# The first FFN product of chunks 16 to 19 as seven half products, in a kernel with its order written out by hand

## The chip, the cores and the metric

The kernel runs on one core of a Trainium2 chip. The time is in device microseconds (us) for one execution. Engines are named as the profile names them: PE (TensorE, matmuls), PEld (its weight loads), DVE (VectorE), ACT (ScalarE), POOL (GpSimd) and SP (SyncE, which here only issues DMAs).

## The reference

A linear attention with decay, then a feed-forward net with a squared ReLU:

```python
for t in range(S):                      # per batch and head, D = 64, S = 768
    state = gamma * state + outer(k[t], v[t])
    y[t] = scale * (q[t] @ state)
x = y, heads side by side               # 3072 tokens x 512
h = maximum(x @ w_in, 0)                # 512 x 2048
out = (h * h) @ w_out                   # 2048 x 512
```

There are 4 batches and 8 heads; inputs and output are float32, the matmuls take bf16.

## The kernel before

The 3072 tokens are 24 chunks of 128. Four chunks in a row form a group g (0 to 5), which shares an x tile `xt` (x transposed: 4 blocks of 128 rows x 512 tokens) and a tile of squares `h2` (16 blocks x 512 tokens).

Every step is given to a planner (`Plan.add`) with a name, and `TURNS` lists for each engine the order of all names. PE, DVE, ACT, POOL and SP each work through their list; a step waits on its engine until its inputs are there, and all behind it wait too. The planner gives the four PSUM banks `fps` in that order. The names:

- `ldk/ldq/ldv m` (SP, L701): loads of chunk m; `ck/cq m`: their casts to bf16 (L517 on ACT, L519 on DVE, L521 on POOL); `cv m` (DVE, L711): v with its decay; `X m` (SP, L743): DMA transpose of k and q.
- `V m.n` (PE, L767 to L805): a visit. It applies the state and scores for chunk m into the PSUM tile `yy`, and makes scores and state sums for chunk n in `sc`. Then `P n` (L846), `S n.0`, `S n.1` (L858, L856) and `Y m` (L866) on DVE make the masked scores, the new states and the x tile's columns.
- `F1.b.f` (PE, L979): eight 256-wide matmuls of the first FFN product for block b (two chunks), one bank; `R b.f` (ACT, L986) the ReLU to float32; `Q b.f` (L998 on ACT, L1000 on DVE) the square into `h2`. There are 16 of each for a group.
- `M1.c` to `M7.c` (PE, L1191): the second product for a unit of two chunks (c, c+1) as seven products of halves in the manner of Strassen and Winograd, eight matmuls each, in two banks (A, B). `H1, H2, H5, H6, H7` (DVE, L1166) are sums of squares for them, `e4, cc` (ACT, L1215, L1221), `t1, u1, w, c` (DVE, L1211) put the result together, and `st c.0`, `st c.1` (SP, L1245) store it. `w` frees bank A, `c` bank B.
- For the last group alone (chunks 20 to 23) the first product is done in that manner too (`ffn1_four`): `WI1` to `WI4` (L1032, two halves each) are sums of quarters of w_in, `TX0` to `TX3` (DVE, L1039) sums of x. For each tile t of four, `G1.t` to `G7.t` (PE, L1064) are four matmuls each; they go into two banks of `sc` or `yy` (U, W) and one of `fps` (V). `kc11, kc12, kc22` (ACT, L517) keep a product in float32, `c11, c22, c12` (DVE, L1079) add a second to it, `Qc..` squares the sum: one instruction on DVE (L1091), two on ACT (L1088 ReLU, L1089 square). `R.t` and `Q.t` (L1112, L1118) finish the fourth quarter. The w_in sums lie in the load buffers, the kept products in `yf`.

```python
            mult(2, "W", True)
            mult(1, "U", True)
            kept("c11", "U")
            both("c11", "W", bkeys["W"])
            squared("c11", 0, 0)
            mult(6, "U", False)      # adds to U after kc11 has read it
```

A half product that adds to a bank thus waits for the copy of what was there, and a first one for the bank to be freed.

Of the kernel before, what the change touches and what calls it, by code (L numbers as in the profile page):

```python
# [10 lines left out]
FP32 = mybir.dt.float32  # L11
BF16 = mybir.dt.bfloat16
# [6 lines left out]
class Plan:  # L19
# [47 lines left out]
    def schedule(self, nbanks, max_open, nslots):  # L67
# [176 lines left out]
BLOCKS = [2, 2, 1, 1, 2, 2, 2, 2, 2, 2, 2, 4]  # L244
# [27 lines left out]
FUSED = ()  # L272
# [80 lines left out]
def kernel(  # L353
# [9 lines left out]
    nc = tc.nc  # L363
# [22 lines left out]
    NLD, NBF, NQT, NXT, NH2, NWS, NOSB, NST = 4, 5, 5, 3, 3, 4, 3, 6  # L386
# [38 lines left out]
    osbs = [sb(f"osb{j}", [P, DM], FP32) for j in range(NOSB)]  # L425
    rts = [sb(f"r{j}", [P, 512], FP32) for j in range(NR)]
# [534 lines left out]
    def ffn1(blk):  # L961
# [4 lines left out]
        xt, h2, cols = xts[g % NXT], h2s[g % NH2], slice(u0 * C, u0 * C + n)  # L966
        for f0 in range(0, NFB, per):
# [22 lines left out]
            def relu_square(f0=f0, o1=o1):  # L990
                t = fps[o1["op"]["bank_index"]][:].rearrange("p (u n) -> p u n", u=per)
                nc.vector.scalar_tensor_tensor(out=h2[:, f0 : f0 + per, cols], in0=t, scalar=0.0, in1=t,
                                               op0=ALU.max, op1=ALU.mult)

            def square(on, f0=f0, o1=o1):
# [6 lines left out]
            hk = [f"h{g % NH2}.{u0 + w}.{f0 + u}" for u in range(per) for w in range(nb)]  # L1002
            i0 = pl.add(f"F1.{blk}.{f0}", "PE", per * NCB * (n * 0.4167 + (3 if n > C else 10)) / 1e3, reads, (f"g{grp}",), mm, lat=0.2, bank=("open", grp, False),
                        count=per * NCB, after=openers.get(g - NH2, ()))
            f1_of.setdefault(g, []).append(i0)
            o1["op"] = pl.ops[i0]
            if f"{blk}.{f0}" in FUSED:
                pl.add(f"RQ{blk}.{f0}", "DVE", 0.602, (f"g{grp}",), hk, relu_square,
                       bank=("close", grp), after=twin_users if g == NH2 - 1 else pt_users if g == 1 else ())
                continue  # L1010
# [3 lines left out]
                   after=twin_users if g == NH2 - 1 else pt_users if g == 1 else ())  # L1014

    def ffn1_four(blk):
        g = blk0[blk] // 4
        xt, h2 = xts[g % NXT], h2s[g % NH2]
        xk = [f"xt{g % NXT}.{u}" for u in range(4)]
        part = lambda k, t: xt[:, 2 * k : 2 * k + 2, 256 * t : 256 * t + 256]  # L1020
        ws = lambda h, k, j: w_in_bf[2 * h + j][:, 2 * k : 2 * k + 2, :]
        wkeys = lambda h, j: [f"win{2 * h + j}.{cb}.{e}" for cb in range(NCB) for e in range(2)]
        room = lambda x, slot: ld[x][:, slot, :].bitcast(BF16).rearrange("p (c n) -> p c n", c=2)
        places = {"1": ("k0", "k1"), "2": ("q0", "q1"), "3": ("v0", "v1"), "4": ("k2", "q2")}
        wt = {y + str(j): room(places[y][j][0], int(places[y][j][1])) for y in places for j in range(2)}
        for j in range(2):
            for y, a, b, op in (("1", (1, 0), (1, 1), ALU.add), ("2", "1", (0, 0), ALU.subtract),
                                ("3", (0, 0), (1, 0), ALU.subtract), ("4", (0, 1), "2", ALU.subtract)):
                ops_ = [wt[z + str(j)] if isinstance(z, str) else ws(*z, j) for z in (a, b)]
                reads = [x for z in (a, b) for x in ([f"WI{z}.{j}"] if isinstance(z, str) else wkeys(z[0], j))]  # L1030
                pl.add(f"WI{y}.{j}", WSUM2, 0, reads, (f"WI{y}.{j}", "ld" + places[y][j]),
                       lambda on, o=wt[y + str(j)], ops_=ops_, op=op: (nc.vector if on == "DVE" else nc.gpsimd).tensor_tensor(  # L1032
                           out=o, in0=ops_[0], in1=ops_[1], op=op), lock=BOTH)
        tx_ = xts[(g + 1) % NXT]
        tx = {y: tx_[:, 2 * (y // 2) : 2 * (y // 2) + 2, 256 * (y % 2) : 256 * (y % 2) + 256] for y in range(4)}
        for y, a, b, op in ((0, part(0, 1), part(0, 0), ALU.subtract), (1, part(1, 1), tx[0], ALU.subtract),
                            (2, part(1, 1), part(0, 1), ALU.subtract), (3, part(1, 0), tx[1], ALU.subtract)):
            pl.add(f"TX{y}", {"DVE": 0.341}, 0, xk + ([f"TX{y // 2}"] if y % 2 else []), [f"TX{y}"],
                   lambda on, y=y, a=a, b=b, op=op: (nc.vector if on == "DVE" else nc.gpsimd).tensor_tensor(  # L1039
                       out=tx[y], in0=a, in1=b, op=op), lock=BOTH, after=f1_of.get(g - 2, ()))  # L1040
        room32 = yf[:].rearrange("p a n -> p (a n)").rearrange("p (z y n) -> p z y n", z=2, y=3)
        left = {1: lambda f, k: ws(0, 0, f // 4)[:, k, C * (f % 4) : C * (f % 4) + C],
                2: lambda f, k: ws(0, 1, f // 4)[:, k, C * (f % 4) : C * (f % 4) + C],
                4: lambda f, k: ws(1, 1, f // 4)[:, k, C * (f % 4) : C * (f % 4) + C]}
        for i, y in ((3, "4"), (5, "1"), (6, "2"), (7, "3")):
            left[i] = lambda f, k, y=y: wt[y + str(f // 4)][:, k, C * (f % 4) : C * (f % 4) + C]
        right = {1: part(0, 0), 2: part(1, 0), 3: part(1, 1), 4: tx[3], 5: tx[0], 6: tx[1], 7: tx[2]}
        lkey = {1: lambda j: wkeys(0, j), 2: lambda j: wkeys(0, j), 4: lambda j: wkeys(1, j), 3: lambda j: [f"WI4.{j}"],
                5: lambda j: [f"WI1.{j}"], 6: lambda j: [f"WI2.{j}"], 7: lambda j: [f"WI3.{j}"]}
        rkey = {1: xk[:2], 2: xk[:2], 3: xk[2:], 4: ["TX3"], 5: ["TX0"], 6: ["TX1"], 7: ["TX2"]}  # L1050
        for t in range(4):
            z = t % 2
            both_ = held_by[z]
# [323 lines left out]
```

## Time and profile before

| what | value |
|---|---|
| time, median of three runs | 201.94 us (201.85 to 202.0) |
| the profiled execution | 202.31 us |
| its span, first to last instruction | 200.5 us |
| PE / PEld / DVE / ACT / POOL busy | 191.8 / 158.8 / 159.4 / 134.8 / 38.1 us |
| granted TensorE clock | 0.991 of full speed |
| bytes read and written | 27.26 and 6.29 MB |
| first product, chunks 0 to 19 (L979) | 704 matmuls |
| first product, chunks 20 to 23 (L1064) | 112 matmuls |

Busy times overlap, and a matmul's duration holds the depth of PE's pipeline, so durations of single matmuls must not be added up. The last product ends at about 197.1 us, and three DVE steps, a store and its landing follow.

### The profile page before, as it was taken

To read this page: it belongs to the slowest core of one execution; us is meant where nothing else is said; L and a number is where in the kernel's file an instruction comes from. 1 tells how busy PE (TensorE), PEld (TensorE's weight loads), DVE (VectorE), ACT (ScalarE), POOL (GpSimd) and SP (SyncE) were. 2 spreads that over 40 slices of the span, in tenths; PEclk is the share of its full clock that TensorE was granted. 3 is DMA by queue.
4 is the path that set the end of the run, shared out by engine and by line. 5 is a ranking of instruction groups with operands and counts; after the bars stand their busy time and mean duration, and the time that the engine had idled before them with its cause. 6 is when DMAs were issued, how large, how long until landed. Compare 5 with 4: busy or idle time off the path is not lost.

```text
span 200.5 us, 7020 instructions
## 1 busy us (share of the span) xinstructions
PE 191.8 (96%) x3011; PEld 158.8 (79%) x3016; DVE 159.4 (79%) x301; ACT 134.8 (67%) x239; POOL 38.1 (19%) x59
## 2 busy tenths in 40 slices
PE   8987999899999999999999999999999999999993
PEld 5654797674587888888888888888888888888882
DVE  3486449668849998969989888969899699999962
ACT  8564899778882784697885488386588418887601
POOL 6541352220102101201311012112010920000000
PEclk9996999999999999999999999999999999999999
DMA  5999999999999999999999999998992111100233
GB/s 158 290 312 320 345 345 336 352 264 215 245 162 241 207 248 204 256 170 250 128 146 243 205 246 214 210 225 191 157 194 54 56 56 56 52 0 28 83 105 105
DMA packets 97935, 38.46 MB, mean 192 GB/s; under 512 B 81008, under 2 KB 94320, under 8 KB 97904
## 3 DMA queue, kind: packets, MB, share of 16 engines
q1 hardware_dynamic: 97760, 37.89, 87.0%
q8 instruction: 23, 0.38, 0.8%
q10 hardware_dynamic: 144, 0.13, 0.2%
q14 instruction: 8, 0.07, 0.2%
HBM read 27.26 MB, written 6.29 MB: 167 GB/s over the span
## 4 chain that ended last, share of the span: by engine, by line
PE 65%; DMA 22%; SPq 6%; POOL 2%; issue 1%; ACT 1%; DVE 1%; DVEq 0%; POOLq 0%; ACTq 0%
PE fps L1191 27%; PE fps L979 21%; DMA kn<-in_k_dram 8%; DMA qkT<-kqs 7%; PE fps L1269 6%; DMA wst<-in_moe_w_in_dram 4%; DMA qn<-in_q_dram 4%; SPq L954 3%; PE yy L1064 2%; PE sc L1064 2%; SPq L536 2%; PE fps L1064 2%; PE yy L767 2%; PE sc L793 1%; PE yy L782 1%
## 5 line engine op out<-in xcount | busy, mean ns | idle before, releaser
L979 PE MATMUL fps<-xt,w_in 128*128 128x256 bf16 (+1 forms) x704 | 79.0, 266 | 0.9 <-ACT w_in L517 0.9
L979 PEld LDWEIGHTS <-w_in 128*128 128x128 bf16 x704 | 63.1, 99 | 9.4 <-ACT w_in L517 1.5
L986 ACT ACTIVATE r<-fps 128x512 f32<-128x512 f32 x80 | 47.1, 593 | 25.9 <-PE fps L979 19.8
L1191 PE MATMUL fps<-wst,h 128*128 128x256 bf16 x320 | 39.2, 273 | 0.0
L998 ACT ACTIVATE h<-r 128x512 bf16<-128x512 f32 x57 | 35.3, 628 | 1.1
L1191 PEld LDWEIGHTS <-h 128*128 128x128 bf16 x320 | 31.0, 98 | 3.9
L1191 PEld LDWEIGHTS <-wst 128*128 128x128 bf16 x240 | 23.3, 98 | 2.8
L711 DVE TENSOR_TENSOR vs<-vn,vf 128x512 bf16<-128x512 f32 x20 | 14.5, 724 | 7.4 <-DMA vn<-in_v_dram 7.4
L1166 DVE TENSOR_TENSOR wst<-h 128x1024 bf16<-128x1024 bf16 x30 | 19.4, 686 | 0.7 <-ACT h L998 0.4
L1191 PE MATMUL fps<-w_out,wst 128*128 128x256 bf16 x160 | 19.9, 273 | 0.0
L1000 DVE TENSOR_TENSOR h<-r 128x512 bf16<-128x512 f32 x23 | 16.2, 721 | 2.7 <-ACT r L986 2.7
L521 POOL CAST kqs<-kn 128x512 bf16<-128x512 f32 x12 | 8.4, 696 | 49.9 <-DMA kn<-in_k_dram 31.9
L521 POOL CAST kqs<-qn 128x512 bf16<-128x512 f32 x11 | 7.2, 653 | 43.6 <-DMA qn<-in_q_dram 30.9
L1269 PE MATMUL fps<-w_out,h 128*128 128x512 bf16 x59 | 14.4, 379 | 1.0 <-DVE w_out L519 0.6
L866 DVE TENSOR_TENSOR xt<-yy,yf 128x512 bf16<-128x512 f32 x19 | 13.1, 687 | 2.1 <-PE yy L782 1.9
L858 DVE TENSOR_TENSOR state<-sc,state 128x256 bf16<-128x256 f32 x33 | 13.8, 419 | 0.4
L1166 DVE TENSOR_TENSOR h<-h 128x1024 bf16<-128x1024 bf16 x20 | 13.7, 706 | 0.1
L846 DVE TENSOR_TENSOR pt<-sc,cmask 128x512 bf16<-128x512 f32 x20 | 13.6, 681 | 0.0
L1211 DVE TENSOR_TENSOR wu<-fps,wu 128x512 f32<-128x512 f32 (+1 forms) x16 | 9.1, 571 | 4.7 <-ACT osb L1221 2.5
L1221 ACT ACTIVATE osb<-fps 128x512 f32<-128x512 f32 x10 | 6.0, 596 | 8.6 <-PE fps L1191 8.6
L1269 PEld LDWEIGHTS <-h 128*128 128x128 bf16 x64 | 5.9, 98 | 6.8 <-issue 0.9
L1191 PE MATMUL fps<-wst,wst 128*128 128x256 bf16 x80 | 10.4, 273 | 0.0
(120 smaller groups left out, 245.3 us busy)
## 6 DMA issues: line engine op xcount, KB each, us to landing
qn<-in_q_dram SPq DMA_DIRECT2D x20, 256.0 KB, 5.0
kn<-in_k_dram SPq DMA_DIRECT2D x20, 256.0 KB, 5.6
vn<-in_v_dram SPq DMA_DIRECT2D x20, 256.0 KB, 5.5
out_dram<-osb SPq DMA_DIRECT2D x19, 256.0 KB, 3.8
wst<-in_moe_w_out_dram SPq DMA_DIRECT2D x4, 1024.0 KB, 10.2
wst<-in_moe_w_in_dram SPq DMA_DIRECT2D x4, 512.0 KB, 8.5
wst<-in_moe_w_in_dram SPq DMA_DIRECT2D x2, 1024.0 KB, 8.2
kn<-in_k_dram SPq DMA_DIRECT2D x2, 512.0 KB, 4.2
```

The lines of the kernel that those rows point to most:

```text
L521: nc.gpsimd.tensor_copy(o, t)
L711: lambda: nc.vector.tensor_tensor(out=o[:], in0=t.rearrange("s (h d) -> s h d", h=H), in1=vf[:, i, :, None].to_broadcast([P, H, D]), op=AL ...
L846: lambda: nc.vector.tensor_tensor(out=pt[:], in0=sc[:, :, 0:256].rearrange("s g (p t) -> s g p t", p=NJ), in1=cmask[:, None, None, :].to_b ...
L858: f = lambda cc=cc, j1=j1, j0=j0: nc.vector.tensor_tensor(out=sts[j1][:], in0=cc, in1=sts[j0][:], op=ALU.add)
L866: lambda: nc.vector.tensor_tensor(out=xt[:, :, u * C : u * C + C].rearrange("s p (g t) -> s g p t", g=2), in0=yy[:, :, 0:256].rearrange("s ...
L979: nc.tensor.matmul(ps[:, u * n : u * n + n], lhsT=w_in_bf[j][:, cb, c * P : (c + 1) * P], rhs=xt[:, cb, cols], start=(cb == 0), stop=(cb = ...
L986: nc.scalar.activation(o, t, AF.Relu)
L998: nc.scalar.activation(hv, rv, AF.Square)
L1000: (nc.vector if on == "DVE" else nc.gpsimd).tensor_tensor(out=hv, in0=rv, in1=rv, op=ALU.mult)
L1166: lambda on, o=a[name], x=a[x], y=a[y], op=op: (nc.vector if on == "DVE" else nc.gpsimd).tensor_tensor(out=o, in0=x, in1=y, op=op), lock=BOTH)
L1191: nc.tensor.matmul(ps[:, 256 * half : 256 * half + 256], lhsT=a[left][:, f], rhs=right(f), start=(first and f == 0), stop=True, skip_group ...
L1269: nc.tensor.matmul(ps[:, 0:w], lhsT=h2[:, fb, u * C : u * C + C], rhs=w_out_bf[j][:, c, ns], start=(fb == 0), stop=(fb == NFB - 1))
```

## The change

Chunks 16 to 19 are now one block of four too, so that `ffn1_four` runs for groups 4 and 5 (steps are named `G1.t.4`, `kc11.t.4` and so on, or `.5`). `F1`, `R` and `Q` of their two blocks of two go. In detail:

- For group 4, U and V are both banks of `fps`, and the second product goes to V rather than to a third bank W. The last group keeps U and W in `sc` and `yy`.
- The sums of w_in are made once and used for both groups. `WI1`, `WI2` and `WI4` lie in the tile of squares `h2[2]`, which held the squares of chunks 8 to 11; `WI3` overwrites its first operand in w_in. Group 4's kept products take the rest of that tile and one new tile, three places in turn. Group 5's squares go into `h2[0]` (`HOF`).
- There are two x tiles instead of three; three of the four sums of x have a new small tile, the fourth overwrites a quarter of x.
- From about the visit V15.16 on, the lists of all engines are written anew. All four chunks of group 4 must have been visited before most of its half products, and the visits stand earlier among the products. The casts of k and q of chunks 19 to 22 go to ACT, those of chunk 23 to POOL. Loads, transposes and stores on SP from ldk18 on have another order. The last two products of the kernel, M7.22 and M6.22, change places, and so do c1.22 and c2.22.

PE's list from V17.18 to V22.23, before and after:

```
V17.18 F1.8.10 M1.12 F1.8.12 F1.8.14 M4.12 F1.9.0 F1.9.8 M5.12 V18.19 F1.9.2 F1.9.4 M2.12 F1.9.6
F1.9.10 M6.12 M7.12 V19.20 F1.9.12 F1.9.14 M3.14 F1.10.0 F1.10.2 M4.14 F1.10.8 F1.10.6 V20.21 F1.10.10
F1.10.4 M1.14 M5.14 M2.14 F1.10.12 V21.22 F1.10.14 M6.14 M3.16 M7.14 V22.23

V17.18 M7.10 F1.8.0 F1.8.8 M4.12 F1.8.10 V18.19 F1.8.12 G1.0.4 M1.12 G2.0.4 M5.12 V19.20 M2.12 M6.12
G5.0.4 G6.0.4 M7.12 G3.0.4 G1.1.4 G7.0.4 M3.14 G2.1.4 G6.1.4 M4.14 G5.1.4 G4.0.4 G7.1.4 V20.21 G3.1.4
G4.1.4 M5.14 G1.2.4 G2.2.4 M2.14 M1.14 G5.2.4 G6.2.4 V21.22 G3.2.4 G1.3.4 G7.2.4 M6.14 G2.3.4 G6.3.4
M7.14 G5.3.4 G4.2.4 G7.3.4 V22.23
```

ACT's list after, from cc.12 to kc11.0.5, and SP's from ldk18 to ldk23:

```
cc.12 ck22 kc22.0.4 kc12.0.4 Qc11.0.4 kc11.1.4 Qc12.0.4 Qc22.0.4 kc12.1.4 e4.14 kc22.1.4 R.0.4 Qc11.1.4
Qc22.1.4 R.1.4 kc11.2.4 Qc12.1.4 Q.0.4 cc.14 kc22.2.4 kc12.2.4 Qc11.2.4 kc11.3.4 Qc12.2.4 Qc22.2.4
kc12.3.4 kc22.3.4 Qc11.3.4 Q.1.4 R.2.4 R.3.4 Q.2.4 Q.3.4 kc11.0.5

ldk18 ldq19 ldq18 X17 ldk19 ldk20 ldv18 ldq20 X18 ldv19 ldv20 X19 ldq21 st8.0 ldk21 X20 ldq22 ldk22
st10.0 ldv23 ldv21 ldv22 st10.1 X21 X22 ldq23 ldk23
```

The diff, cut to its core:

```diff
-BLOCKS = [2, 2, 1, 1, 2, 2, 2, 2, 2, 2, 2, 4]
+BLOCKS = [2, 2, 1, 1, 2, 2, 2, 2, 2, 4, 4]
+HOF = (0, 1, 2, 0, 1, 0)
...
-    NLD, NBF, NQT, NXT, NH2, NWS, NOSB, NST = 4, 5, 5, 3, 3, 4, 3, 6
+    NLD, NBF, NQT, NXT, NH2, NWS, NOSB, NST = 4, 5, 5, 2, 3, 4, 3, 6
...
+    txs = sb("tx", [P, 3, 2, 256], BF16)
+    spare = sb("spare", [P, 512], FP32)
...
-        xt, h2, cols = xts[g % NXT], h2s[g % NH2], slice(u0 * C, u0 * C + n)
+        xt, h2, cols = xts[g % NXT], h2s[HOF[g]], slice(u0 * C, u0 * C + n)
...
+    before = {g: max([x for x in range(g) if HOF[x] == HOF[g]], default=None) for g in range(NM // 4)}
+    fours = [x // 4 for x, n in zip(blk0, blocks) if n == 4]
+    ws = lambda h, k, j: w_in_bf[2 * h + j][:, 2 * k : 2 * k + 2, :]
+    wkeys = lambda h, k, j: [f"win{2 * h + j}.{2 * k + x}.{e}" for x in range(2) for e in range(2)]
+    room16 = h2s[2]
+    wt = {(y, j): room16[:, 4 * x + 2 * j : 4 * x + 2 * j + 2, :] for x, y in enumerate("124") for j in range(2)}
+    wt.update({("3", j): ws(1, 0, j) for j in range(2)})
+    wtkey = {(y, j): [f"WI{y}.{j}"] if y != "3" else wkeys(1, 0, j) for y in "1234" for j in range(2)}
+    room32 = [room16[:, 12 + 2 * x : 14 + 2 * x, :].rearrange("p a n -> p (a n)").bitcast(FP32) for x in range(2)] + [spare[:]]
+    room_last = yf[:].rearrange("p a n -> p (a n)").rearrange("p (x n) -> p x n", x=6)
+
+    def sums_of_w_in():
+        old = lambda *fs: [f"h2.{u}.{f}" for u in range(4) for f in fs] if HOF[2] == 2 else []
+        for j in range(2):
+            for x, y, a, b, op in ((0, "1", (1, 0), (1, 1), ALU.add), (1, "2", "1", (0, 0), ALU.subtract),
+                                   (2, "4", (0, 1), "2", ALU.subtract), (3, "3", (0, 0), (1, 0), ALU.subtract)):
+                ops_ = [wt[z, j] if isinstance(z, str) else ws(*z, j) for z in (a, b)]
+                reads = [k for z in (a, b) for k in (wtkey[z, j] if isinstance(z, str) else wkeys(*z, j))]
+                pl.add(f"WI{y}.{j}", WSUM2, 0, reads, wtkey[y, j] + (old(4 * x + 2 * j, 4 * x + 2 * j + 1) if y != "3" else []),
+                       lambda on, o=wt[y, j], ops_=ops_, op=op: (nc.vector if on == "DVE" else nc.gpsimd).tensor_tensor(
+                           out=o, in0=ops_[0], in1=ops_[1], op=op), lock=BOTH, after=twin_users if y != "3" else ())
+
+    turn32 = [0]
...
-        tx_ = xts[(g + 1) % NXT]
-        tx = {y: tx_[:, 2 * (y // 2) : 2 * (y // 2) + 2, 256 * (y % 2) : 256 * (y % 2) + 256] for y in range(4)}
+        tx = {0: txs[:, 0], 1: txs[:, 1], 2: part(0, 1), 3: txs[:, 2]}
...
-            pl.add(f"TX{y}", {"DVE": 0.341}, 0, xk + ([f"TX{y // 2}"] if y % 2 else []), [f"TX{y}"],
+            pl.add(f"TX{y}.{g}", {"DVE": 0.341}, 0, xk + {0: [], 1: ["TX0"], 2: ["TX0"], 3: ["TX1"]}[y], [f"TX{y}"],
...
-        room32 = yf[:].rearrange("p a n -> p (a n)").rearrange("p (z y n) -> p z y n", z=2, y=3)
...
+            if last:
+                z = t % 2
+                fixed = {"U": held_by[z][:, 0, :], "W": held_by[z][:, 1, :]}
+                bkeys = dict.fromkeys("UW", [("sc", "yy")[z] + x for x in "01"])
+            else:
+                fixed, bkeys = {}, {"U": [f"gU{g}.{t}"]}
+            bkeys["V"] = [f"gV{g}.{t}"]
...
+            c, ck, cold = {}, {}, {}
+            for x, name in enumerate(("c11", "c12", "c22")):
+                if last:
+                    c[name], ck[name], cold[name] = room_last[:, 3 * (t % 2) + x], f"last{3 * (t % 2) + x}", []
+                else:
+                    y = turn32[0] % 3
+                    turn32[0] += 1
+                    c[name], ck[name] = room32[y], f"room{y}"
+                    cold[name] = [f"h2.{u}.{12 + 2 * y + e}" for u in range(4) for e in range(2)] if y < 2 and HOF[2] == 2 else []
...
+            if last:
+                mult(2, "W", True)
+                mult(1, "U", True)
+                kept("c11", "U")
+                both("c11", "W")
+                squared("c11", 0, 0)
+                mult(6, "U", False)
+                kept("c12", "U")
+                mult(5, "V", True, True)
+                kept("c22", "V")
+            else:
+                mult(1, "U", True, True)
+                kept("c11", "U")
+                mult(2, "V", True, True)
+                both("c11", "V")
+                squared("c11", 0, 0)
+                mult(6, "U", False)
+                kept("c12", "U")
+                mult(5, "V", True)
+                kept("c22", "V")
...
+            while blocks[done] == 4 and before[m // 4] is not None and done2 < 4 * before[m // 4] + 4:
+                finish(done2)
+                done2 += 2
```

More of the change, by code (lines that the diff above doesn't have):

```diff
@@ L1000, in square @@
                     (nc.vector if on == "DVE" else nc.gpsimd).tensor_tensor(out=hv, in0=rv, in1=rv, op=ALU.mult)
-            hk = [f"h{g % NH2}.{u0 + w}.{f0 + u}" for u in range(per) for w in range(nb)]
+            hk = [f"h{HOF[g]}.{u0 + w}.{f0 + u}" for u in range(per) for w in range(nb)]
             i0 = pl.add(f"F1.{blk}.{f0}", "PE", per * NCB * (n * 0.4167 + (3 if n > C else 10)) / 1e3, reads, (f"g{grp}",), mm, lat=0.2, bank=("open", grp, False),
-                        count=per * NCB, after=openers.get(g - NH2, ()))
-            f1_of.setdefault(g, []).append(i0)
+                        count=per * NCB, after=openers.get(before.get(g), ()))
             o1["op"] = pl.ops[i0]
[L1007 to L1010, printed above, removed]
             i0 = pl.add(f"R{blk}.{f0}", RELU, 0, (f"g{grp}",), (f"r{grp}",), relu, bank=("close", grp), slot=("open", grp))
@@ L1016, in ffn1_four @@
+    turn32 = [0]
     def ffn1_four(blk):
         g = blk0[blk] // 4
[L1018 removed]
+        last = g == NM // 4 - 1
+        if g == fours[0]:
+            sums_of_w_in()
+        xt, h2 = xts[g % NXT], h2s[HOF[g]]
         xk = [f"xt{g % NXT}.{u}" for u in range(4)]
         part = lambda k, t: xt[:, 2 * k : 2 * k + 2, 256 * t : 256 * t + 256]
[L1021 to L1022 removed]
@@ L1023, in ffn1_four @@
[L1023 to L1033, printed above, removed]
@@ L1060, in mm, with at, mult @@
+            bkeys["V"] = [f"gV{g}.{t}"]
+            tag = f"{t}.{g}"
+            pool = lambda bank, end, tag=tag, fixed=fixed: None if bank in fixed else (end, (bank, tag), False) if end == "open" else (end, (bank, tag))
+            def at(bank, fixed=fixed, o1=o1):
+                return fixed[bank] if bank in fixed else fps[o1[bank]["bank_index"]][:]
+            def mult(i, bank, first, opens=False, t=t, at=at, bkeys=bkeys, o1=o1, tag=tag, pool=pool):
                 def mm():
-                    ps = banks[bank] if bank != "V" else fps[o1["op"]["bank_index"]][:]
+                    ps = at(bank)
@@ L1076, in both @@
-            def both(name, x, reads, t=t, c=c, banks=banks, o1=o1, **kw):
-                get = lambda: banks[x] if x != "V" else fps[o1["op"]["bank_index"]][:]
-                pl.add(f"{name}.{t}", "DVE", 0.602, reads, [f"{name}.{z}"],
-                       lambda: nc.vector.tensor_tensor(out=c[name], in0=get(), in1=c[name], op=ALU.add), **kw)
-            def squared(name, hh, tt, t=t, c=c):
+                i0 = pl.add(f"G{i}.{tag}", "PE", 0.437, lkey[i](t // 2) + rkey[i], bkeys[bank], mm, lat=0.2,
+                            count=4, bank=pool(bank, "open" if opens else "use"))
@@ new lines, in kept, with both @@
+            def kept(name, bank, c=c, ck=ck, cold=cold, at=at, bkeys=bkeys, tag=tag, pool=pool):
+                pl.add(f"k{name}.{tag}", KEPT, 0, bkeys[bank], [ck[name]] + cold[name],
+                       lambda on: copy_on(on, c[name], at(bank)), bank=pool(bank, "use"),
+                       after=y_made if last else twin_users)
+            def both(name, x, end="use", c=c, ck=ck, at=at, bkeys=bkeys, tag=tag, pool=pool):
+                pl.add(f"{name}.{tag}", "DVE", 0.602, bkeys[x], [ck[name]],
+                       lambda: nc.vector.tensor_tensor(out=c[name], in0=at(x), in1=c[name], op=ALU.add),
+                       bank=pool(x, end))
@@ L1120, in square @@
                     nc.vector.tensor_tensor(out=o, in0=rv, in1=rv, op=ALU.mult)
-            pl.add(f"Q.{t}", SQUARE, 0, (f"rw{t}",), [f"h{g % NH2}.{w}.{8 + 2 * t + u}" for u in range(2) for w in range(2)],
-                   square, slot=("close", ("f1w", t)), lock=BOTH)
+            pl.add(f"Q.{tag}", SQUARE, 0, (f"rw{tag}",), [f"h{HOF[g]}.{w}.{8 + 2 * t + u}" for u in range(2) for w in range(2)],
+                   square, slot=("close", ("f1w", tag)), lock=BOTH)
     def rows(m):
@@ L1262, in ffn2 @@
                 for j in range(4):
-                    reads = [f"h{g % NH2}.{u}.{4 * j + c}" for c in range(4)] + [f"wout{j}.{c}.{h}" for c in range(4) for h in range(2)]
+                    reads = [f"h{HOF[g]}.{u}.{4 * j + c}" for c in range(4)] + [f"wout{j}.{c}.{h}" for c in range(4) for h in range(2)]
                     def mm(j=j, o1=o1, h2=h2, u=u, ns=ns, w=w):
```

71 lines of the change are left out of this document (22 added, 49 removed), and 57 rows, old and new, of the table TURNS.

## The prediction

> **What bounds the kernel now.** I read the page first: its busy shares and its 40 slices.
>
> ```profile
> PE 191.8 (96%) x3011; PEld 158.8 (79%) x3016; DVE 159.4 (79%) x301; ACT 134.8 (67%) x239; POOL 38.1 (19%) x59
> PE   8987999899999999999999999999999999999993
> ```
>
> TensorE (PE) has no slice under 90% from the tenth on. A busy share can hide pipelining, so next comes the chain of waits in order of time (start, length, what), which gives the pace at which matmuls are really issued:
>
> ```profile
> 171.91 0.87 PE fps L1064 x8
> 172.78 0.44 PE yy L1064 x4
> 182.39 13.11 PE fps L1191 x120
> ```
>
> 13.11 / 120 = 109.3 ns for a matmul of 256 columns; eight take 0.874 us, four 0.437, whether they are the products of the second FFN (L1191) or of the half products (L1064). The mean durations in the page's groups (some 270 ns) hold the pipeline's depth and would make the saving 2.5 times too large. From 106 us to the last product PE's rows follow each other at this pace with no gap but the visits, 0.755 us each. So the end moves by what PE no longer does, unless PE begins to wait.
>
> The windows (PE, weight loads, DVE, ACT, POOL, clock, DMA) say who stands close behind it:
>
> ```profile
> 150.00:155.00 5.00, 5.00 (x80) 4.48 (x67) 4.96 (x11) 4.13 (x9) 0.08 (x1) 1.00 0.31 56
> 170.00:175.00 5.00, 5.00 (x48) 4.50 (x46) 4.58 (x8) 4.26 (x9) 0.00 (x0) 1.00 0.15 52
> ```
>
> VectorE (DVE) and ScalarE (ACT) are 85 to 99% busy where the half products of chunks 20 to 23 run. The clock is 1.00, so nothing is to be had there.
>
> **What the change removes.** The first product of chunks 16 to 19 is 16 groups of eight matmuls (128); seven half products for four tiles, four matmuls each, are 112. 16 x 109.3 ns = 1.75 us less on PE, all in the stretch without gaps. Early work is ordered as before up to about 108 us on every engine, so nothing moves there.
>
> [...]
>
> **What it adds.** For chunks 16 to 19, ACT and DVE had 16 ReLUs and 16 squares. Now they have 12 copies to keep a product, 12 additions, 12 squares of a sum, 4 ReLUs, 4 squares, and 4 sums of x. Prices, from ACT's timeline:
>
> ```profile
> 167.20 0.59 ACT L517 ACTIVATE yf<-yy 128x512 f32<-128x512 f32 x1
> 167.68 0.61 ACT L517 ACTIVATE yf<-sc 128x512 f32<-128x512 f32 x1
> 186.20 0.62 ACT L1088 ACTIVATE yf<-yf 128x512 f32<-128x512 f32 x1
> 186.86 0.63 ACT L1089 ACTIVATE h<-yf 128x512 bf16<-128x512 f32 x1
> 187.39 0.61 ACT L1088 ACTIVATE yf<-yf 128x512 f32<-128x512 f32 x1
> ```
>
> Start to start, a copy or ReLU from PSUM costs 0.485 us, a ReLU-and-square pair 1.19, a plain square 0.53; on DVE any 512-wide step starts 0.60 after the one before it. What ACT gains over the rest of the kernel is some 13.6 us, DVE 4 (it hands squares and a cast to ACT). None of this is on the path unless PE waits for it, so I laid PE's new order out without waits, from the visit V14.15 at 105.44 on, and asked at each place whether its inputs and its PSUM bank are there. A step of ACT starts 0.24 us after PE's last issue, one of DVE 0.15 (V17.18 ended at 127.87 by this count and its Y row began at 128.04).
>
> DVE: from V15.16 to V22.23 it has 38.9 us of steps in PE's 42.0 (before: 36.7 in 46.3). It waits for PE at several visits, so it holds.
>
> ACT is the tight one. From kc22.0.4 (it can start at 137.9, after G5.0.4) to Q.3.4 it has 16 copies and ReLUs (7.76), 10 pairs (11.90), 4 squares (2.12) and one 0.28: 22.06 us, to 159.96, its result about 160.1. M4.16, which reads that result, is due on PE at 160.35. ACT thus has no idle time for 22 us and arrives 0.2 us early. On the way kc12.3.4 is ready at 155.85, where G7.3.4 is due at 155.79: a wait of 0.1. G3.2.4 and G1.3.4 (the latter wants the bank that w.14 frees) have 0.1 to 0.2 to spare. I take 0.15 us of waits. The bounds: nothing, if copies overlap a little better; and 2 us, if each of the 21 copies and pairs in the run costs 0.1 us more than the dense rows (half a semaphore hop of PE to ACT).
>
> **The moved feed.** V18.19 is due on PE at 130.5 instead of 134.9, V19.20 at 134.7 instead of 141.7, because the half products need all four chunks. Each visit needs a transposed k and q by DMA:
>
> ```profile
> 121.26 2.13 SPq L743 DMA_TRANSPOSE qkT<-kqs  x1
> 127.75 1.91 SPq L743 DMA_TRANSPOSE qkT<-kqs  x1
> DMA to landing us min/median/max: 3.1/4.2/5.9
> ```
>
> These are X18 and X19, landing 4.3 and 4.2 later. SP is the issuer and runs into the DMA queue there: from ldk18 at 111.48 to X18 it passes nine issues, 1.09 us each, to X19 fourteen, 1.16 each. In the new order eight stand ahead of X18, eleven ahead of X19 and fifteen ahead of X20 (three stores and later loads go behind them). So X18 is issued at 120.2 to 120.8 and lands by 125.1, due 125.4; X19 lands by 128.5, due 130.5; X20 by 133.1, due 134.7. Cover shrinks from 1.6, 3.0 and 7 us to 0.3, 2.0 and 1.6. I take 0.1 us for X18; the slowest landing, 5.9, would make it 1.3. The casts of chunks 19 to 22 go from POOL to ACT; at those places ACT still has idle time (R8.0 would wait for PE anyway), and behind them stand ReLUs and copies of products that PE issues later. What waits for the delayed stores st8.0, st10.0 and st10.1 are the sums of units 12 and 14 into the same tiles, some 5 us later.
>
> **The weight sums** are eight as before, now needed from 137 on: five on DVE at 0.60 (in the DVE sum), three on POOL at 2.13, with the casts of chunk 23 behind them. POOL is done near 135 and those casts have until their loads come near 144; X23 then lands near 149, V22.23 is due 156.2. One DVE step (WI3.1) runs beside a POOL sum. The nearest rows:
>
> ```profile
> 148.84 0.67 POOL L521 CAST kqs<-kn 128x512 bf16<-128x512 f32 x1 [8.06 <-ACT h L998]
> 148.95 1.10 DVE L1032 TENSOR_TENSOR vn<-w_in,w_in 128x1024 bf16<-128x1024 bf16 x1
> 149.97 0.68 DVE L1032 TENSOR_TENSOR qn<-kn,w_in 128x1024 bf16<-128x1024 bf16 x1
> ```
>
> 0.42 us for the collision; TX0 behind it would be ready at 137.1, and G5.0.4 is due at 137.2: nothing, but without this cover it is 0.4. Two x tiles for three and the square tiles anew cost no wait: chunk 16's x overwrites what F1.6.14 read some 20 us earlier, and chunk 20's squares go where M7.14 reads last, before G2.0.5.
>
> **The tail.** The last two products change places, so the last store is issued by ACT, not SP. In the trace before, ACT's issue stood 0.23 us behind DVE's end, SP's 0.09: 0.15 more.
>
> **Sum.** -1.75 + 0.15 (ACT) + 0.10 (X18) + 0.15 (tail) = -1.35 us. The profiled execution took 202.31 (span 200.5 and 1.8 around it), 0.37 above the median; I carry the difference over: 201.94 - 1.35 = 200.6.
>
> **Rivals.** *ACT becomes the bound* (slower). Place: 138 to 160 us. ACT has 22.06 us for PE's 22.7, so every 0.03 us more on each of its 31 steps costs about 0.9 us, less the 0.2 to spare. At 0.1 on the copies and pairs PE waits 1.9 us more than forecast: 202.5. It is slower than before from 1.35 us of further waits on. For it: no stretch of the trace has ACT busy 22 us on end, and a late copy holds PE at once, since the next half product adds into the same bank. Against it: its dense runs keep their 0.485 and 1.19.
>
> *The feed is late.* If X18 to X20 land no earlier than before (125.6, 131.9, 134.6), V18.19 waits 1.4 us, and what follows has that as slack: 200.6 + 1.3 = 201.9, no change. A landing of 5.9 at X19 on top gives 203.
>
> *PE is not the bound.* If PE could issue faster than it does and something beside it set the pace, the 16 matmuls would be worth nothing and the added 0.4 us would stay: 202.3. The even 109.3 ns through products of both kinds speaks against it. [...]
>
> **How the numbers follow.** Forecast 0.74; ACT bound 0.14; late feed 0.08; PE not the bound 0.04. This kernel's runs lie within 0.15 us, so about 0.2% (0.4 us) is what can be told from no change: faster is under 201.54, slower over 202.34. Faster is the forecast alone, 0.74. The late feed gives 0.05 to no change and 0.03 to slower, PE not the bound 0.03 and 0.01, and the ACT bound is slower: same 0.08, slower 0.18. The forecast's own range is 200.1 (no waits, no tail cost) to 201.4; the range that leaves out no more than 2 in 10 reaches into the ACT case, to 202.6.
>
> **What would show it.** In the profile after: 112 matmuls in place of 128 for these chunks, PE's issue pace still 109.3 ns; the last product's end near 195.6 instead of 197.1; V19.20 near 135; ACT without idle time from 138 to 160. Gaps of PE released by ACT between 143 and 160 would show the ACT rival, gaps at visits released by the transposes near 125 to 135 the feed. Wrong would be any PE wait over half a us, or a pace that changes.

## The result and the profile after

The changed kernel takes 200.66 us (median of 22 runs, 199.92 to 204.75) beside 201.94 (22 runs, 201.48 to 203.78) of the kernel before on the same chip: a ratio of 0.9937 with a 95% interval of 0.9917 to 0.9958, 1.28 us less. Now and then an execution takes well over a per cent longer than the others of its kernel, as the 204.75 did; the ratios leave out such executions, the medians do not. The profiled execution took 200.48 us (span 198.7), 1.83 less than the one of before.

The page of the changed kernel, its busy line and PE's, DVE's and ACT's slices:

```profile
PE 189.6 (95%) x2995; PEld 157.0 (79%) x3000; DVE 160.9 (81%) x309; ACT 145.4 (73%) x262; POOL 34.1 (17%) x54
PE   8886999999999999999999999999999999999993
DVE  3486439777849898978999479989999998999962
ACT  8564789968882684687887868498999999798101
```

PE has 16 instructions fewer and is still full from the fifth slice to the last but one. ACT's busy time grew by 10.6 us, and its slices read 9 where group 4's half products run.

The chain of waits (start, length, what) answers to the pace shown before, and it holds the only wait of PE between 125 us and the last product that the kernel before has not:

```profile
153.95 0.87 PE fps L1226 x8
154.82 0.45 PE fps L1080 x4
155.28 0.03 ACTq L524
155.30 0.44 ACT h L524
155.75 0.04 issue
155.79 0.60 PE fps L1080 x4
180.60 13.12 PE fps L1226 x120
```

The pace has not changed: 13.12 / 120 = 109.3 ns. L1080 are the half products, L1226 the second product. At 155.79 begins G7.3.4. Four matmuls at that pace from about 155.10 would have let it begin at 155.54, so PE stood for 0.25 us behind a copy of ACT (L524, kc12.3.4). On ACT's timeline that copy (155.16) stands behind the pair Qc22.2.4; the two rows above it are the square of Qc11.2.4 and the copy kc11.3.4, which the account of ACT further down needs:

```profile
151.63 0.63 ACT L1114 ACTIVATE h<-h 128x512 bf16<-128x512 f32 x1
152.29 0.60 ACT L524 ACTIVATE h<-fps 128x512 f32<-128x512 f32 x1
...
153.98 0.61 ACT L1113 ACTIVATE spare<-spare 128x512 f32<-128x512 f32 x1
154.62 0.63 ACT L1114 ACTIVATE h<-spare 128x512 bf16<-128x512 f32 x1
155.16 0.58 ACT L524 ACTIVATE h<-fps 128x512 f32<-128x512 f32 x1
```

The windows (PE, weight loads, DVE, ACT, POOL, clock, DMA share, GB/s), first of the kernel before:

```profile
138.00:149.00 11.00, 11.00 (x160) 9.72 (x159) 10.11 (x18) 7.71 (x16) 1.39 (x3) 1.00 0.96 180
149.00:160.00 11.00, 11.00 (x230) 9.39 (x232) 9.26 (x19) 7.75 (x14) 5.58 (x4) 1.00 0.32 70
```

and of the kernel after:

```profile
138.00:149.00 11.00, 11.00 (x160) 9.71 (x159) 10.88 (x21) 10.78 (x21) 1.74 (x2) 1.00 0.90 167
149.00:160.00 11.00, 10.91 (x227) 9.15 (x224) 10.85 (x21) 10.84 (x22) 0.00 (x0) 1.00 0.35 93
```

ACT went from 15.46 to 21.62 us of 22, as forecast. DVE went from 19.37 to 21.73: it is as full as ACT.

**One stretch for every comparison.** Executions differ ahead of the change as well: V14.15's scores began at 105.93 us in the profile of before, at 105.61 in that of after, at 105.05 to 108.07 in the experiments. I therefore measure from there to the start of the last of the 256-wide matmuls. That stretch took 91.03 us before (196.96 - 105.93, with 768 such matmuls) and 89.56 after (195.17 - 105.61, with 752). The 1.47 us are 16 x 109.3 ns = 1.75, less 0.25 for G7.3.4, less 0.03 that lies at the visits, whose lengths differ by some hundredths. The other 0.36 of the 1.83 lie ahead of V14.15 (0.32) and behind the last matmul (0.04).

### The profile page after: what moved, and what is told of

Same layout as the page of the kernel before. It is cut to its first block, busy times and chain, and to the rows that moved or that the text cites. A ratio compares the mean times of both kernels' runs of the same rounds, so it can differ in the third digit from the quotient of the medians.

```text
span 198.7 us, 7019 instructions
## 1 busy us (share of the span) xinstructions
PE 189.6 (95%) x2995; PEld 157.0 (79%) x3000; DVE 160.9 (81%) x309; ACT 145.4 (73%) x262; POOL 34.1 (17%) x54
## 4 chain that ended last, share of the span: by engine, by line
PE 74%; DMA 16%; SPq 5%; POOL 1%; DVE 1%; issue 1%; ACT 1%; DVEq 0%; ACTq 0%
PE fps L1226 30%; PE fps L986 20%; DMA kn<-in_k_dram 8%; PE fps L1080 8%; PE fps L1304 6%; DMA wst<-in_moe_w_in_dram 4%; DMA qkT<-kqs 4%; SPq L961 3%; PE yy L1080 2%; PE sc L1080 2%; PE yy L774 2%; SPq L543 2%; PE yy L789 1%; PE sc L800 1%; PE sc L812 1%; POOL w_in L528 1%
## 5 line engine op out<-in xcount | busy, mean ns | idle before, releaser
L986 PE MATMUL fps<-xt,w_in 128*128 128x256 bf16 (+1 forms) x576 | 62.9, 263 | 1.3 <-ACT w_in L524 1.1
L993 ACT ACTIVATE r<-fps 128x512 f32<-128x512 f32 x64 | 37.3, 591 | 16.0 <-PE fps L986 15.4
L1226 PE MATMUL fps<-wst,h 128*128 128x256 bf16 x320 | 40.1, 273 | 0.0
L1226 PEld LDWEIGHTS <-h 128*128 128x128 bf16 x320 | 30.9, 98 | 3.9
L1000 ACT ACTIVATE h<-r 128x512 bf16<-128x512 f32 x48 | 29.6, 626 | 0.9
L1226 PEld LDWEIGHTS <-wst 128*128 128x128 bf16 x240 | 23.3, 98 | 2.8
L1226 PE MATMUL fps<-w_out,wst 128*128 128x256 bf16 x160 | 20.3, 273 | 0.0
L718 DVE TENSOR_TENSOR vs<-vn,vf 128x512 bf16<-128x512 f32 x20 | 13.9, 699 | 5.8 <-DMA vn<-in_v_dram 5.7
L1002 DVE TENSOR_TENSOR h<-r 128x512 bf16<-128x512 f32 x16 | 11.2, 709 | 3.7 <-ACT r L993 3.7
L528 POOL CAST kqs<-kn 128x512 bf16<-128x512 f32 x10 | 6.9, 691 | 41.9 <-DMA kn<-in_k_dram 36.1
L1080 PEld LDWEIGHTS <-w_in 128*128 128x128 bf16 x128 | 12.5, 98 | 1.7 <-issue 0.3
L1201 DVE TENSOR_TENSOR h<-h 128x1024 bf16<-128x1024 bf16 x20 | 13.6, 702 | 0.0
L853 DVE TENSOR_TENSOR pt<-sc,cmask 128x512 bf16<-128x512 f32 x20 | 13.6, 680 | 0.0
L528 POOL CAST kqs<-qn 128x512 bf16<-128x512 f32 x8 | 4.9, 613 | 36.6 <-DMA qn<-in_q_dram 36.6
```

The source lines that it names most:

```text
L528: nc.gpsimd.tensor_copy(o, t)
L718: lambda: nc.vector.tensor_tensor(out=o[:], in0=t.rearrange("s (h d) -> s h d", h=H), in1=vf[:, i, :, None].to_broadcast([P, H, D]), op=AL ...
L853: lambda: nc.vector.tensor_tensor(out=pt[:], in0=sc[:, :, 0:256].rearrange("s g (p t) -> s g p t", p=NJ), in1=cmask[:, None, None, :].to_b ...
L986: nc.tensor.matmul(ps[:, u * n : u * n + n], lhsT=w_in_bf[j][:, cb, c * P : (c + 1) * P], rhs=xt[:, cb, cols], start=(cb == 0), stop=(cb = ...
L993: nc.scalar.activation(o, t, AF.Relu)
L1000: nc.scalar.activation(hv, rv, AF.Square)
```

## Experiments

Theory: PE issues without a gap, so its 16 matmuls are the gain; one place behind ACT gives 0.25 of it back. Rivals: ACT or DVE sets the time between 138 and 160 us; the feed of X18 to X20 does; PE's matmuls are worth less than their pace; the tail costs something. All times are medians; ratios are against the kernel before on the same chip.

**The changed kernel again.**

> The changed kernel once more, as the measure for the others of this set on the same chip. Both theories: 1.3 us under the kernel before (ratio 0.9937), one wait of PE at G7.3.4 of about 0.25 us, released by ACT.

200.78 us (8 runs), ratio 0.9923 (0.9896 to 0.9949). The result stands. The profile is of an execution of 203.90 us: it has the wait at G7.3.4 (0.25), but also two that the first profile has not, of 0.2 us at V17.18 (X18 landed at 127.99) and 0.76 at V19.20 (X20 at 138.12), in a stretch of 90.50. Most of what it took longer came ahead: its V14.15 began at 108.07.

**The matmuls back, and nothing else.** In each first half product that opens a bank, the opening matmul is issued twice: 16 more matmuls with their weight loads, no more work for the other engines.

```diff
-    nc.tensor.matmul(...)
+    for _ in range(2 if first and u == 0 and k == 0 and (not last or i == 2) else 1):
+        nc.tensor.matmul(...)
```

> 16 matmuls more: the first matmul of each opening half product of group 4 (12) and of G2 of group 5 (4) is issued twice, so that PE has as many 256-wide matmuls as before the change. Theory (PE's pace is the bound): 16 x 109.3 ns = 1.75 us slower than the changed kernel, less the 0.25 us of the wait at G7.3.4 that the later PE no longer meets: 1.5 to 1.75, so 0.1 to 0.5 us slower than the kernel before. Rival (PE is not the bound, something beside it sets the pace): under 0.5 us slower than the changed kernel.

202.06 us (12 runs), ratio 0.9989 (0.9970 to 1.0008): the gain is gone, with 1.28 us more than the control in the medians. The stretch is 91.05 us, 1.49 more than after: 1.75 less the 0.25 at G7.3.4, which no longer occurs because ACT has time to come. Its chain ends on PE at the same pace:

```profile
181.72 13.12 PE fps L1227 x120
```

So a matmul costs its pace here, and PE is the bound. Weight loads are busy for 9.71 of 11 us (88%) in the first window of after above, and still the run shows no headroom on PE.

**The copy first.** On ACT, kc12.3.4 goes ahead of the ReLU and square Qc22.2.4.

```diff
-Qc12.2.4 Qc22.2.4 kc12.3.4 kc22.3.4
+Qc12.2.4 kc12.3.4 Qc22.2.4 kc22.3.4
```

> ACT's list: kc12.3.4 goes ahead of the pair Qc22.2.4, all else as in the changed kernel. Theory (PE's pace sets the time, and ACT, which has no idle time from 138 to 160 us, costs one wait): kc12.3.4 is ready 1.2 us earlier, the wait of 0.25 us at G7.3.4 goes, nothing new is late (kc22.3.4 then ends where it did), 0.2 to 0.25 us faster than the changed kernel, last product at 195.0 instead of 195.3. Rival (ACT bounds the whole stretch): the work of ACT is the same, so the wait comes back later in the stretch, at M4.16 at the latest, and the time stays within 0.05 us.

200.40 us (6 runs), ratio 0.9913 (0.9885 to 0.9941), 0.4 under the changed kernel on the same chip, with intervals that overlap. The expected 0.20 to 0.25 is only in part there: on PE's timeline G7.3.4 begins without a wait, and a smaller one of 0.11 stands behind the visit V22.23 (four matmuls at 157.41, the next at 157.97 instead of 157.86):

```profile
155.80 0.60 PE L1080 MATMUL fps<-tx,w_in 128*128 128x256 bf16 x4
156.23 0.60 PE L1080 MATMUL fps<-xt,w_in 128*128 128x256 bf16 x4
...
157.41 0.61 PE L1080 MATMUL fps<-xt,h 128*128 128x256 bf16 x4
157.97 0.60 PE L1080 MATMUL fps<-tx,w_in 128*128 128x256 bf16 x4
```

So the move gains 0.14 at these two places. This execution's stretch is longer all the same, 90.61, by two waits for the feed: 0.27 at V17.18, whose scores want X18 (issued 120.28, landed 125.13), and 0.92 at V19.20, whose scores (L800) want X20 (the row counts the idle time alone, 0.76):

```profile
135.46 0.32 PE L800 MATMUL sc<-qkT 64*64 64x64 bf16 x16 [0.76 <-DMA qkT<-kqs]
```

**More work for ACT.** One square of group 4 (Q.0.4) is done twice on ACT.

```diff
-    nc.scalar.activation(o, rv, AF.Square)
+    for _ in range(2 if tag == "0.4" else 1):
+        nc.scalar.activation(o, rv, AF.Square)
```

> ACT squares Q.0.4 twice: one step of 0.53 us more in the stretch where ACT has no idle time. Theory (ACT is full there, arriving 0.1 to 0.2 us ahead of PE at most places): PE waits 0.4 us at G3.2.4 and the wait at G7.3.4 grows with it, 0.5 us slower than the changed kernel in all. Rival (ACT has slack there and the wait at G7.3.4 has another cause): no change, within 0.1 us.

201.36 us (12 runs), ratio 0.9963 (0.9942 to 0.9984), 0.6 more than the control beside it. The two squares took ACT 1.18 us to the next step's start, where the one took 0.52: 0.66 more, and not the 0.53 of the expectation.

```profile
149.38 1.27 ACT L1154 ACTIVATE h<-r 128x512 bf16<-128x512 f32 x2
150.56 0.58 ACT L1257 ACTIVATE osb<-fps 128x512 f32<-128x512 f32 x1
```

PE's timeline has it at two places, after the visit V21.22 and at G7.3.4:

```profile
151.67 0.60 PE L1080 MATMUL fps<-xt,h 128*128 128x256 bf16 x4 [0.55 <-ACT spare L524]
...
156.81 0.60 PE L1080 MATMUL fps<-xt,w_in 128*128 128x256 bf16 x4 [0.18 <-ACT h L524]
```

Counted from start to start, the first holds PE 0.61 longer than a visit otherwise does, and the second is 0.34 instead of 0.25. Its stretch is 91.15 us: 89.56 + 0.61 + 0.09 + 0.90 (to 0.01), the last a wait for X20 at V19.20 as in the run before. So ACT has nothing to spare: 0.66 us more of work costs 0.70.

**More work for DVE.** One of the 1024-wide additions for unit 14, H5.14, is done twice, which takes DVE 0.72 us more from start to start.

```diff
-    nc.vector.tensor_tensor(out=o, in0=x, in1=y, op=op)
+    for _ in range(2 if name == "H5" and c0 == 14 else 1):
+        nc.vector.tensor_tensor(out=o, in0=x, in1=y, op=op)
```

> DVE makes H5.14 twice: one step of 0.60 us more near 143 us. The prediction's reading (DVE's sum to V22.23 is 38.9 us of PE's 42, it holds): at most 0.3 us slower than the changed kernel, by c22.1.4 ahead of G4.1.4, which has 0.35 us to spare, and nothing later. Rival (DVE is busy 21.8 of 22 us from 138 to 160 and is a second full engine there): 0.5 to 0.6 us slower.

200.61 us (12 runs), ratio 0.9953 (0.9925 to 0.9980): no measurable difference to the changed kernel. In the trace DVE's addition c22.1.4 begins 0.61 us later than in the changed kernel, both counted from V14.15, and G4.1.4 waits for it:

```profile
145.32 0.60 PE L1080 MATMUL fps<-tx,w_in 128*128 128x256 bf16 x4 [0.25 <-DVE spare L1103]
```

PE loses 0.41 there by its starts, the wait at G7.3.4 is gone since ACT gains that time, and the stretch is 89.74, 0.18 more. DVE is as busy as ACT but is late less: at this place it had some 0.2 (0.61 - 0.41) to give, where ACT has none.

**A late feed.** SP issues X19 after the loads that stood behind it.

```diff
-ldv20 X19 ldq21 st8.0 ldk21 X20
+ldv20 ldq21 st8.0 ldk21 X19 X20
```

> SP's list: ldq21, st8.0 and ldk21 go ahead of X19 instead of behind it. Theory (the loads and transposes pass the DMA queue at about 1.1 us each and have little cover left): X19 lands 3.3 us later, near 132.2, V18.19 is due at 130.3, so PE waits about 1.9 us there; X20 follows at once and lands near 133.3 to 134, so V19.20 does not wait more; 1.7 to 2.0 us slower than the changed kernel, slower than the kernel before. Rival (the feed still has the cover of before, 3 us and more): no change.

202.28 us (12 runs), ratio 1.0027 (0.9991 to 1.0063). The profiled execution is the fastest of them (201.0). Counted from V14.15, X19 was issued 2.3 us later than in the changed kernel (124.84 - 105.05 against 123.07 - 105.61), and V18.19 waited 1.10 us from start to start:

```profile
131.04 0.32 PE L800 MATMUL sc<-qkT 64*64 64x64 bf16 x16 [0.92 <-DMA qkT<-kqs]
```

Its stretch is 90.65, which is 89.56 + 1.10 to 0.01. A transpose 2.3 us later thus takes 1.1 us in the trace and 1.5 in the medians (202.28 against the control's 200.78), all of the gain; the expected 1.7 to 2.0 was more. The rival of the late feed is a real one: the changed kernel's own cover is enough in some executions and not in others.

**The tail as before.** M7.22 and M6.22, and c1.22 and c2.22, back in their old order.

```diff
-... w.22 c2.22 c1.22          # DVE
-M6.22 M7.22                   # PE
+... w.22 c1.22 c2.22
+M7.22 M6.22
```

> The last two products and the two DVE steps behind them in the order of before (M7.22, M6.22; c1.22, c2.22), all else as in the changed kernel. The prediction's term for the tail: 0.15 us faster than the changed kernel, since SP issues the last store 0.09 us behind DVE, ACT 0.23. Rival (the trace after shows 0.67 us from the last product to the last store, 0.66 before): no change, within 0.05 us.

200.84 us (12 runs), ratio 0.9951 (0.9925 to 0.9978), no difference. The timelines' last two store issues, of before, of after and of this run, one fence for each:

```profile
197.41 0.37 ACTq L1238 DMA_DIRECT2D out_dram<-wu  x1
197.74 0.34 SPq L1238 DMA_DIRECT2D out_dram<-wu  x1
```

```profile
195.61 0.34 SPq L1273 DMA_DIRECT2D out_dram<-wu  x1
195.95 0.37 ACTq L1273 DMA_DIRECT2D out_dram<-wu  x1
```

```profile
195.49 0.37 ACTq L1273 DMA_DIRECT2D out_dram<-wu  x1
195.82 0.34 SPq L1273 DMA_DIRECT2D out_dram<-wu  x1
```

The second issue begins 0.33 or 0.34 after the first, whichever queue comes first: each follows 0.02 to 0.04 us behind the end of its DVE step (197.38 and 197.71 before, 195.59 and 195.91 after), and those two steps are that far apart. The last issue stands 0.78 us behind the start of the last matmul in all three (197.74 - 196.96, 195.95 - 195.17, 195.82 - 195.04).

**An earlier feed.** X20 was late in three profiles (the control's, the copy's and that of more work for ACT), so SP issues it ahead of a store.

```diff
-X19 ldq21 st8.0 ldk21 X20
+X19 ldq21 X20 ldk21 st8.0
```

> The changed kernel with one move on the queue of SP: the transpose X20 and the load of chunk 21's k go ahead of a store (st8.0, 1.92 us of issue), so X20 is issued at about 125.7 instead of 128.2 and the k load at its old time. Theory (the shorter feed cover costs part of the executions: V19.20's scores wait 0.8 to 0.9 us for X20 in some, nothing in others): that wait is gone in every profile, executions without it keep their time, and the median comes down by 0.1 to 0.5 us, to 200.2 to 200.6. Rival (the spread between executions is of the chip, and X20 only shows it): the median stays at 200.7 to 200.8, and another wait stands in the place of V19.20's. Against the move: the store is issued 2.5 us later; where the sum of unit 12 into its tile waits for it, ACT or DVE stops near 134 and PE loses up to 1 us.

200.82 us (6 runs), ratio 0.9934 (0.9908 to 0.9959): no gain. X20 was issued at 125.6 and landed at 130.7, due 134.8; the stretch is 89.55. The store pays for it: st8.0, issued at 129.07, landed at 132.87, and t1.12, which overwrites the tile that it reads, began at 132.97, 0.88 us after e4.12 instead of the 0.41 in the changed kernel. PE lost no more than 0.04 behind that.

**The earlier feed and the copy first.** Both moves together.

> The same move on SP's queue, and on ACT the copy kc12.3.4 one place earlier, ahead of the ReLU and square Qc22.2.4. If both waits that the trace of the changed kernel shows (0.25 us at G7.3.4, 0.8 to 0.9 at V19.20 in part of the executions) are of these two places, the median is 0.3 to 0.6 us below the changed kernel's, 200.1 to 200.5, with no wait over 0.15 us on PE between 125 us and the last product. Rival (the work of ACT and DVE is the limit between 138 and 160 us, so that what one place gains the next loses): no more than 0.1 us below the feed alone.

201.71 us (12 runs), ratio 0.9965 (0.9938 to 0.9993), a miss. Its profile is of an execution of 204.88 us, and it shows what the move can do. On DVE's timeline t1.12 waits for the store:

```profile
131.49 0.68 DVE L853 TENSOR_TENSOR pt<-sc,cmask 128x512 bf16<-128x512 f32 x1
135.98 0.42 DVE L1246 TENSOR_TENSOR osb<-fps,e 128x256 f32<-128x256 f32 x1 [3.81 <-DMA out_dram<-osb]
```

st8.0 was issued at 130.27 there. PE's next second product wants the bank that t1.12 and the step after it free, so PE stood too, and then something else followed. The row of PE, and its windows (busy, clock, DMA share, GB/s):

```profile
136.46 1.03 PE L1226 MATMUL fps<-w_out,wst 128*128 128x256 bf16 x8 [2.60 <-DVE osb L1246]
```

```profile
134.00:136.40 2.40, 0.00 (x0) 1.00 1.00 210
136.40:138.00 1.60, 1.54 (x71) 0.95 1.00 244
138.00:141.20 3.20, 3.20 (x35) 0.50 1.14 254
141.20:144.00 2.80, 2.80 (x27) 0.99 0.88 120
```

After 2.60 us without a matmul, and 1.4 us after the matmuls had come back, the granted clock fell to 0.50 for 3.41 us (137.83 to 141.24; the windows above cut it at both ends), and matmuls came each 213 ns. The stretch of 94.05 is 4.6 us over that of the best run below: 2.76 for the wait, 1.58 for the clock and 0.27 for X18 at V17.18, all from start to start. Whether this is why the median is higher is not shown, since the other executions have no trace; the move was not used again.

**The changed kernel a third time.**

> The changed kernel itself, on the same chip as the two kernels with the earlier feed: 200.5 to 200.8 us if its earlier medians (200.66, 200.78) hold here. By the theory of the feed some of its executions show a wait of 0.8 to 0.9 us at V19.20; a profile of one execution shows it or not.

200.74 us (11 runs), ratio 0.9934 (0.9914 to 0.9954). The profiled execution took 201.56, yet its stretch is 89.56 with no wait but the one at G7.3.4: all of the 1.1 us that it is slower than the first profile came ahead of V14.15.

**The feed ordered anew, with the store early.** The store goes ahead of X20, chunk 21's loads behind, and their casts on ACT later.

```diff
-X19 ldq21 st8.0 ldk21 X20                      # SP
+X19 st8.0 X20 ldq21 ldk21
-Q8.8 cq21 e4.12 R8.12 kc11.0.4 Q8.10 ck21 Q8.12 cq22   # ACT
+Q8.8 e4.12 R8.12 kc11.0.4 Q8.10 Q8.12 cq21 ck21 cq22
```

> The changed kernel with chunk 20's feed ahead of chunk 21's, and the store before both: SP's order is X19, st8.0, X20, ldq21, ldk21; on ACT the casts cq21 and ck21 stand after Q8.12, where their loads will have come. X20 is issued near 127 instead of 128.2, and st8.0, whose landing releases the tile that t1.12 writes near 132.4, at 125 to 126 in place of 125.7 to 128. Theory (part of the executions lose time at these two covers, 0.55 to 2.1 us for X20 and 0.55 to 0.8 for st8.0): no wait at V19.20, t1.12 never held by the store, and the median 0.1 to 0.4 us under the changed kernel's 200.66 to 200.78. Rival (the executions' spread comes from elsewhere, much of it already from before 60 us): the median stays within 0.1 of 200.7. Against it: ldq21 lands near 134, and if the casts hold ACT past 137.4 the first copy of the half products is late, and ACT carries that for 20 us: 201 to 201.5.

200.91 us (12 runs), ratio 0.9949 (0.9923 to 0.9975). X20 landed at 132.3, due 136.0, so its cover is 3.7 us, and there is no wait at V19.20 or for the store. The stretch is 89.66, and the execution (201.87) lost 1.1 us at V14.15, whose X15 came late; that place is as before the change. The rival is right: what the executions differ by is not made at X20 alone, and the median does not move.

**The new feed order and the copy first.**

> The same order of feed and casts, and on ACT the copy kc12.3.4 one place earlier. Theory: 0.1 to 0.25 us under the feed order alone, since the wait of 0.25 at G7.3.4 becomes one of 0.11 behind V22.23: 200.1 to 200.5. Rival: no difference between the two, as DVE is as full as ACT there.

200.50 us (12 runs), ratio 0.9930 (0.9900 to 0.9961), 0.4 under the order of the feed alone, again with overlapping intervals; that run's two middle times are 200.64 and 201.18, so its median is loose by a quarter of a us either way. The stretch is the shortest of all, 89.43: 0.25 less at G7.3.4, 0.12 more behind V22.23. By the traces the copy is worth 0.13 us; the medians of the changed kernel and its feed orders (200.40 and 200.50 with it, 200.66 to 200.91 without) point the same way by more than that, but the one with X20 ahead of the store does not (201.71 with it, 200.82 without), and the runs do not settle how much. Both versions beat the kernel before; that they beat the changed kernel is not shown.

## Why the prediction was right, step by step

**The matmuls, -1.75: right, and shown.** Putting 16 back cost 1.49 us in the stretch, and 1.75 with the 0.25 that they hid. *PE is not the bound* fell with that.

**ACT, +0.15: the right place, 0.25.** Of the places named, only G7.3.4 waited; the step "ready at 155.85, where G7.3.4 is due at 155.79: a wait of 0.1" was mis-sized by 0.15. From the start of kc22.0.4 to that of kc12.3.4 ACT took 17.57 us (137.59 to 155.16), where the prediction's prices give 17.34 (12 copies and ReLUs, nine pairs, a square and e4.14). Two copies account for it: kc11.1.4 and kc11.3.4 stand right behind a pair Qc11 whose kept product they overwrite (three places in turn), and begin 0.66 us after the start of its square (151.63 to 152.29, and 139.23 to 139.90) where the copy behind another pair begins 0.54 after (154.62 to 155.16). The prediction asked of each copy whether its product and bank were there, not whether its place was free. This is read from the trace; no run moved those two copies. No cover takes the error up, as the 0.66 us of more work that cost 0.70 show. *ACT becomes the bound* did not happen, but was near: scaled from that one run, the 1.35 us of waits from which it decides are about 1.3 us more on ACT (1.35 x 0.66 / 0.70, an estimate).

**DVE "holds": true by 0.2 us only.** The step took 38.9 us of work against 42.0 as room. It counted the stretch from V15.16 on, and not the 22 us from 138 on, in which DVE is busy 21.73. A sum over the stretch that matters would have put a second rival beside ACT.

**The feed, +0.10 at X18: a cost of some executions, and the larger one missed.** In the first profile X18 landed at 124.1 (1.3 us of cover instead of 0.3), since it was issued at 119.6 and not at 120.2 to 120.8; with the copy first it was issued at 120.28, and V17.18 lost 0.27 us to it. X20, to which 1.6 us of cover and no cost was given, is the tighter one: it landed 4.5 us after its issue in the first profile, at 132.7, due 134.75, but 6.0 after it in the run with more work for ACT (129.04 to 135.05), where V19.20 lost 0.9 us. Three of the eight profiles with this order on SP have such a wait, of 0.76 to 0.92 us, which is the prediction's own sign of being wrong (a wait of PE over half a us). The step that failed is that the slowest landing of before, 5.9, was held against X18 and X19 and not against X20.

**The stores: no cost, as forecast, but by far less room.** "Some 5 us later" was counted from the issue. From landing to use, st8.0 has 0.6 us (issued 127.93, landed 131.59, t1.12 at 132.20, in the run with the copy first). Issued at 129.07 it held t1.12 for some 0.5 us, and at 130.27 DVE stood for 3.81.

**The weight sums, 0, and 0.42 for a collision: none.** POOL's last sum ended at 134.46, WI3.1 on DVE began after it and took its usual 0.68 us; the timelines of POOL and of DVE:

```profile
132.32 2.14 POOL L1032 TENSOR_TENSOR h<-w_in,h 128x1024 bf16<-128x1024 bf16 x1
```

```profile
134.61 0.68 DVE L1032 TENSOR_TENSOR w_in<-w_in,w_in 128x1024 bf16<-128x1024 bf16 x1
```

The prediction gave this no weight in the sum, so nothing hung on it.

**The tail, +0.15: wrong, 0.** The 0.23 for ACT and 0.09 for SP were not a price of a queue: in the rows of before, both issue 0.03 us behind the DVE step that they wait for.

**Other readings.** ACT's busy time grew by 10.6 us and DVE's by 1.5, not by 13.6 and 4; no wait hung on those sums. The first of the two windows that the prediction shows lies ahead of the half products (the first begins at 162.2), and ACT is 83% busy in it. The runs do not lie within 0.15 us: that was three of them, and the 22 lie between 201.48 and 203.78.

So the sum of -1.35 became -1.28 in the medians with the tail's term too high by 0.15 and ACT's too low by 0.10, and with waits at X18 and X20 in part of the executions in place of 0.10 in all. The main term and its mechanism were right; that the total came within 0.07 is partly luck, since these errors offset each other.

## What to carry to other kernels

Where an engine issues without gaps, as PE does here, removed instructions are worth their pace (109.3 ns each; putting the 16 back cost 1.49 us, and 1.75 with the wait that they hid), and the rest of the estimate is a list of single places: lay the new order out and name each step that is due close to its input (G7.3.4, forecast to wait 0.1 us, waited 0.25; V19.20, forecast to have 1.6 us of cover, waited up to 0.92). Count the fullness of the neighbours over the very stretch in which they must keep up (DVE is busy 21.73 of the 22 us from 138 on), and the cover of a buffer from the landing of the store that reads it (0.6 us for st8.0, not 5). To compare two executions, measure from a point ahead of the change that both share, and not from the start (V14.15's scores began at 105.05 to 108.07 us).

## What was not expected of the hardware

- **The clock after an idle PE.** 2.60 us without a matmul, in the run with the earlier feed and the copy first, were followed by a granted clock of 0.50 for 3.41 us. Idle times of 0.76 us (the copy first, at V19.20) and 0.92 us (the late feed, at V18.19) were not: the mean clock of those two executions is 0.991, as in the first profile, where the one stretch at 0.50 lies early (18.99 to 22.40 us). Nor does the idle time alone decide. From 15.50 to 18.99 us PE is busy for 2.10 us and idle for no more than 0.96 us on end in the profile after, and that stretch at 0.50 for 3.41 us follows; in the profile of before one from about 17.0 to 20.4 us begins inside an idle time of 0.88 us (16.60 to 17.48). In the run with more work for ACT PE is busy for 2.03 us from 15.50 to 18.99, and the clock is 1.00 there and in the mean of the whole execution. What decides is not shown.
- **A transpose's landing.** X20 landed 4.5 us after its issue in one execution and 6.1 in another of the same kernel (129.45 to 135.51); with the store ahead of it and the loads behind it, 3.3 (127.48 to 130.78, and 128.96 to 132.31).
- **A collision of casts.** POOL's cast of chunk 23's k took 1.13 us where it began just behind the DVE step cv22 (147.28, 0.68 us), beside 0.61 for the one before it. A cast at 97.80 in the same profile, during which another such step (cv) began at 97.97, took its usual 0.61, and the DVE step 0.99 beside the 0.68 of cv22. In both the one that began second took longer; no run tested it.

```profile
146.41 0.61 POOL L528 CAST kqs<-qn 128x512 bf16<-128x512 f32 x1 [11.95 <-DMA qn<-in_q_dram]
147.31 1.13 POOL L528 CAST kqs<-kn 128x512 bf16<-128x512 f32 x1 [0.29 <-DMA kn<-in_k_dram]
```
